# Earlier loads of a tail, casts on other engines and a new order of steps in a fused attention and MLP kernel

## The chip, the cores and the metric

The kernel runs on one core of a Trainium2 chip. The core has a matrix engine (TensorE, PE in the profile), a vector engine (VectorE, DVE), a scalar engine (ScalarE, ACT), a general engine (GpSimd, POOL) and a sync engine (SyncE, SP) that here only issues transfers. Transfers are carried by 16 DMA engines. The metric is the device time of one execution in microseconds; the median of several executions is given.

## The reference

There are 8 batches of 8 heads, 576 tokens and 64 dimensions a head. Attention is causal with a window of 64 tokens, and its output, with the heads side by side (512 numbers a token), goes through a layer norm, an MLP with a hidden width of 2048, and a residual add.

```python
scores = scale * np.matmul(q, k.transpose(0, 1, 3, 2))
mask = (rel >= 0) & (rel < 64)               # rel = query position - key position
attn = softmax(np.where(mask, scores, -1e9))
x = np.matmul(attn, v)                       # then heads side by side: (8, 576, 512)
xn = (x - mu) / np.sqrt(var + 1e-06) * g_ln
out = x + np.maximum(xn @ w_ch1, 0.0) @ w_ch2
```

## The kernel before

**Groups.** The 576 tokens of a batch are cut into 512 and a tail of 64. The kernel has nine groups of 512 tokens: group g below 8 is the first 512 tokens of batch g, and group 8 gathers the eight tails, two batches to a block of 128 tokens. A block of the attention is called a step j (0 to 3); of group 8, step i is "tail i", with the last 64 tokens of batches 2i and 2i+1. While the MLP of group g runs, the attention of batch b = g + 1 is computed between its matmuls, and in groups 6 and 7 that of the tails too.

**Units and slots.** `mlp_units` returns the matmul units of a group's MLP in order. After unit i the kernel runs what was put into slot i by `at(i, f, ...)`; within a slot, calls run in the order in which they were put there. Everything is written in program order and each engine works through its own list in that order, so a step that waits holds up all that stands behind it on its engine. Groups 2 to 8 have 16 units of the first MLP matrix (L437, `hps`, one chunk of 128 hidden units each) and 14 units of the second (L515, banks `wX`, `wY`, `wZ`), which use sums of the hidden activations (`presum`, L427) and of W2 (`t_weights`, L415). Group 0 splits the first matrix partly by halves of the tokens (L474, `hph`), and so does group 1; their second matrix is plain (L488 and L450, `ch`).

**An attention step.** `s_mm` makes the scores on TensorE (L292) and their exp on ScalarE (L312 or L306); `s_mask` multiplies by the mask on VectorE (L319); `b_step` makes the product with v on TensorE (L335) and, on VectorE, the division by the row sums and the statistics (L338 to L345); `r_step` makes 1/sqrt(var) on ScalarE (L354, L355); `z_step` normalizes on VectorE (L365). z is then transposed, either on TensorE with a copy on ScalarE (`zt_step`, L379 and L382) or by a DMA transpose from SP's queue (`x_step`, L390). `bz(i, ...)` puts `b_step`, `r_step` and `z_step` into slots i, i+1 and i+2.

**q, k and v.** SP loads them in fp32 (L78 to L90, v at L152). They are cast to fp16 by `cp`, on GpSimd (L131) or on ScalarE (L129), and q and k are transposed: for batches 0 to 2 on TensorE (`t_main`, L233, with the copy out at L225 on ScalarE or L227 on VectorE), for the others by DMA from SP's queue (`x_main`, L245 and L251). `pace(t)` is a copy of one column on GpSimd; it makes GpSimd wait until t is written, so that casts come no earlier than a wanted point. A shifted copy of v (`vB`) is made by two DMAs from GpSimd's queue (`make_vB`, L180, L181), for batch 1 by casts (`vB_cur`, `vB_prev`).

**The tails.** `load_tail(i, 0)` issues four loads of q and k from SP (L101, L103), `load_tail(i, 1)` two loads of v (L108). `cast_tail(i, part, act)` casts q (part 0), k (1) or v (2), on ScalarE where act is true. `x_tail(i)` issues two DMA transposes from SP (L261 for q, `tqT`; L262 for k, `tkT`). The staging buffers of q and k exist twice (tail 2 takes that of tail 0), that of v once, so a v load waits for the cast of the v before. The table `TAILS` says in which slot of groups 6 and 7 each of these steps stands. The scores of tail 1 stand in slot 27 of group 6, those of tails 2 and 3 in slots 9 and 13 of group 7.

**W1 and W2.** W1 is loaded in eight pieces (`w1_load`) and cast to fp16 with the norm's gain multiplied in (`w1_cast`: L205 on ScalarE, L207 on VectorE or GpSimd). Pieces 4 to 7 are staged in the space of W2. W2 is loaded in eight pieces through four buffers (`w2_load`, L212) and cast on GpSimd (`w2_cast`, L217); each cast frees the buffer for a later load. `rest_of_loads` holds these casts and loads and those of batch 1 and the q and k of batch 2.

Of the kernel before, what the change touches and what calls it, by code (L numbers as in the profile page):

```python
# [18 lines left out]
def kernel(  # L19
# [10 lines left out]
    nc = tc.nc  # L30
# [92 lines left out]
    def cast_qk(b, half):  # L123
        for x in range(2):
            cast_q(b, x, half)
# [7 lines left out]
    def cast_q(b, x, half, act=False):  # L133
        t = qk32.pop((b, x, half))
        dst = p_in.tile([128, 8, 2, D], FP16, tag=f"qk16_{x}", name=f"qk16_{x}_{b}_{half}")
        qk16[(b, x, half)] = dst
        if b >= NPE and x == 1:
            cp(act, dst[:, :].rearrange("p a e d -> p (a e d)"), t)
            return
        j = 2 if b < 2 else 4  # L140
        cp(act, dst[:, :].rearrange("p (a j) e d -> p a e j d", j=j),
           t[:, :].rearrange("p (a e j d) -> p a e j d", e=2, j=j, d=D))
# [5 lines left out]
    def load_v(b, c0, c1):  # L148
        if c0 == 0:
            v32[b] = p_in.tile([128, 4, H, D], FP32, tag="v32", name=f"v32_{b}", bufs=1)  # L150
        for c in range(c0, c1):
            nc.sync.dma_start(  # L152
                out=v32[b][:, c],
                in_=v[b, :, 128 * c:128 * c + 128, :].rearrange("h s d -> s h d"),
            )

    def cast_v(b, c0, c1, act=False):
        cp(act, vA[b][:, c0:c1, :, 0:D], v32[b][:, c0:c1])
# [50 lines left out]
    def w2_load(i):  # L209
        t = p_wst.tile([128, 2, DM], FP32, tag="wld", name=f"w2s_{i}")  # L210
        wst[("w2", i)] = t
        nc.sync.dma_start(  # L212
            out=t, in_=moe_w_ch2[256 * i:256 * (i + 1), :].rearrange("(c p) d -> p c d", p=128),
        )

    def w2_cast(i):
        nc.gpsimd.tensor_copy(out=w2s[:, 2 * i:2 * i + 2, :], in_=wst.pop(("w2", i)))  # L217
# [152 lines left out]
    def pace(t):  # L370
        nc.gpsimd.tensor_copy(out=tok, in_=t)
# [280 lines left out]
    load_qk(1, 0)  # L652
    for i in range(4):
        w2_load(i)
    cast_qk(1, 0)

    def rest_of_loads():
        for i in range(8):
            w2_cast(i)
            if i < 4:  # L660
                w2_load(i + 4)
        load_v(1, 0, 2)
        cast_v(1, 0, 1)
        cast_v(1, 1, 2)
        load_qk(1, 1)
        load_v(1, 2, 4)
        cast_qk(1, 1)
        cast_v(1, 2, 3)
        cast_v(1, 3, 4)
        load_qk(2, 0)  # L670
        load_qk(2, 1)

    def tail_casts(i, act, *us):
        return tuple((u, cast_tail, i, part, act) for part, u in enumerate(us))

    TAILS = {
        6: ((0, load_tail, 0, 0), (0, load_tail, 0, 1), (6, load_tail, 1, 0), *tail_casts(0, False, 8, 9, 10),
            (10, x_tail, 0), (10, load_tail, 1, 1), *tail_casts(1, True, 17, 18, 19), (18, x_tail, 1),
            (18, s_mm, 8, 0), (19, s_mask, 8, 0), (26, b_step, 8, 0),
            (18, load_tail, 2, 0), (20, load_tail, 2, 1), (20, load_tail, 3, 0),  # L680
            (27, s_mm, 8, 1), (28, s_mask, 8, 1)),
        7: (*tail_casts(2, False, 0, 1, 2), (2, load_tail, 3, 1), (3, x_tail, 2), *tail_casts(3, False, 4, 5, 8),
            (8, x_tail, 3), (2, b_step, 8, 1), (4, zt_step, 8, 0), (7, zt_step, 8, 1),
            (9, s_mm, 8, 2), (11, s_mask, 8, 2), (13, s_mm, 8, 3), (13, b_step, 8, 2),
            (15, s_mask, 8, 3), (17, zt_step, 8, 2), (20, b_step, 8, 3), (25, zt_step, 8, 3)),
    }
    for g in range(NGRP):
# [3 lines left out]
        def at(i, f, *a):  # L691
            slots[min(i, len(slots) - 1)].append((f, a))

        def bz(i, *p):
            at(i, b_step, *p)
            at(i + 1, r_step, *p)
            at(i + 2, z_step, *p)
# [23 lines left out]
        if g == 0:  # L721
            at(0, b_step, 0, 3)
            at(0, z_step, 0, 3)
            at(0, w1_cast, 2, 1, nc.scalar)
            at(0, w1_cast, 3, 1, nc.scalar)
            at(0, w1_cast, 3, 0, nc.scalar, 256, 512)
            at(7, rest_of_loads)
            at(1, zt_step, 0, 2)
            at(2, zt_step, 0, 3)
            for j in range(4):  # L730
                at(3 + j, w1_cast, 4 + j, 0, nc.vector)
                at(3 + j, w1_cast, 4 + j, 1, nc.scalar)
                at(10 + j, r_step, 0, j)
            at(11, t_main, 1, 0, 0, 1)
            at(12, t_main, 1, 1, 0, 1)
            at(17, s_mm, 1, 0)
            at(19, s_mask, 1, 0)
            at(20, s_mm, 1, 1)
            at(22, s_mask, 1, 1)
            at(30, vB_cur, 1, 0, 0)  # L740
            at(30, vB_prev, 1, 0, 1)
            at(32, vB_cur, 1, 1, 0)
            at(33, vB_prev, 1, 1, 0)
            at(33, b_step, 1, 0)
            at(35, b_step, 1, 1)
            at(36, r_step, 1, 0)
            at(37, z_step, 1, 0)
            at(38, r_step, 1, 1)
            at(38, z_step, 1, 1)
            at(41, zt_step, 1, 0)  # L750
            at(42, zt_step, 1, 1)
            at(43, t_main, 1, 0, 1, 0)
            at(44, load_v, 2, 0, 4)
            at(28, alloc_qkT, 2)
            at(28, cast_q, 2, 0, 0)
            at(29, cast_q, 2, 1, 0)
            at(29, make_vB_half, 1)
            at(41, lambda: pace(zT[1][:, 0, 0:1]))
            at(41, cast_q, 2, 0, 1)
            at(43, cast_q, 2, 1, 1)  # L760
        if g == 1:
            at(2, t_main, 1, 1, 1, 1)
            at(4, s_mm, 1, 2)
            at(5, s_mask, 1, 2)
            at(6, s_mm, 1, 3)
            at(7, s_mask, 1, 3)
            bz(7, 1, 2)
            bz(9, 1, 3)
            at(8, t_main, 2, 0, 0, 0)
            at(10, t_main, 2, 1, 0, 0)  # L770
            at(11, zt_step, 1, 2)
            at(13, t_main, 2, 0, 1, 0)
            at(14, zt_step, 1, 3)
            at(15, t_main, 2, 1, 1, 1)
            at(4, alloc_v, 2)
            at(4, alloc_vB, 2)
            for c in range(4):
                at(5 + c, cast_v, 2, c, c + 1)
            at(8, make_vB, 2)
            for j in range(4):  # L780
                at((17, 19, 21, 24)[j], s_mm, 2, j)
                at((18, 20, 22, 25)[j], s_mask, 2, j)
                bz((19, 21, 24, 27)[j], 2, j)
                at((22, 25, 28, 31)[j], zt_step, 2, j)
        if g > 0:
            if g == 1:
                for u, i, c in ((10, 1, 0), (11, 1, 1), (13, 2, 0), (14, 2, 1)):
# [26 lines left out]
        if 0 < g and b + 1 < B:  # L814
            n = b + 1
            e = 3 if g == 1 else 1
            at(e, load_qk, n, 0)
            at(e + 1, load_qk, n, 1)
            at(e + 4, load_v, n, 0, 4)
            if g == 1:  # L820
                at(10, alloc_qkT, n)
                for u, x, half in ((17, 0, 0), (19, 1, 0), (21, 0, 1), (23, 1, 1)):
                    at(u, lambda u=u: pace(hrTs[g][:, 2 * (u - 16), 256:257]))
                    at(u, cast_q, n, x, half)
                at(20, x_main, n, 0)
                at(24, x_main, n, 1)
                at(19, alloc_v, n)
                at(19, alloc_vB, n)
                for u, c, j in ((22, 0, 0), (23, 1, 0), (26, 2, 1), (28, 3, 2)):
                    at(u, (lambda j=j: pace(zT[b][:, 0, 128 * j:128 * j + 1])) if c % 2 == 0 else  # L830
                       (lambda j=j: pace(rss[(b, j)])))
                    at(u, cast_v, n, c, c + 1)
                at(28, make_vB, n)
            else:
                at(3, alloc_qkT, n)
                for u, x, half in ((16, 0, 0), (16, 1, 0), (17, 0, 1), (19, 1, 1)):
                    at(u, cast_q, n, x, half, True)
                at(18, x_main, n, 0)
                at(21, x_main, n, 1)
                at(18, alloc_v, n)  # L840
                at(18, alloc_vB, n)
                for c in range(4):
                    at(21 + c, cast_v, n, c, c + 1, True)
                at(25, make_vB, n)
# [37 lines left out]
```

## Time and profile before

| | us |
|---|---|
| median of 7 executions | 314.52 |
| lowest and highest | 311.74, 318.95 |
| the profiled execution, its own time | 314.01 |
| span of its profile | 312.3 |
| TensorE busy | 293.0 |
| VectorE busy | 192.5 |
| ScalarE busy | 187.7 |
| GpSimd busy | 84.9 |

The span runs from the first to the last instruction; about 1.7 us of the execution's time lie outside of it. The page's groups of instructions give a line, an engine, the operation with its tiles (output, then input), the count, the busy time, the mean of one in ns, and the idle time before them with what ended it:

```profile
L437 PE MATMUL hps<-zT,w1g 128*128 128x512 f16 x480 | 112.5, 382 | 0.9 <-ACT zT L382 0.7
L441 ACT ACTIVATE hrT<-hps 128x512 f16<-128x512 f32 x120 | 71.5, 596 | 45.2 <-PE hps L437 45.2
L319 DVE TENSOR_TENSOR pt<-pt,mask 128x1024 f16<-128x1024 f16 x32 | 22.9, 716 | 31.6 <-ACT pt L312 18.2
L131 POOL CAST qk<-qk 128x1024 f16<-128x1024 f32 x16 | 16.6, 1039 | 13.6 <-DMA qk<-in_q_dram 10.4
```

TensorE's matmuls overlap, so the mean of one is longer than its share of the time. The page's slices of the span (40 of 7.8 us each, a digit for tenths) show the clock that TensorE was granted and the share in which the DMA engines were busy:

```profile
PEclk9999999999999999999999999999999997999998
DMA  7999999999979977998999789979999993003004
```

The DMA engines are busy in almost every slice up to 258 us. One slice has a lower clock, that from 257.6 to 265.4 us.

### The profile page before, as it was taken

The page shows a single profiled execution, that of the slowest core. Times are in us where ns is not written, and L with a number is a line of the kernel's source. Part 1 is how long each engine was busy: PE and PEld are TensorE (multiplying, and loading weights), DVE is VectorE, ACT ScalarE, POOL GpSimd, SP SyncE. Part 2 cuts the span into 40 slices and gives each one's busy share as a digit, 9 for nine tenths or more (in the row PEclk, how much of TensorE's full clock was granted, in tenths as well). Part 3 has the DMA queues.
Part 4 walks back from the last instruction along what each step waited for, and adds up shares of the span by engine and source line. Part 5 has one row for each costly group of instructions (what it writes and reads, how often), then busy time and mean ns, then how long its engine had stood idle before and what let it go on. Part 6 is the DMA issues. An engine that isn't in the chain of part 4 may idle for free.

```text
span 312.3 us, 7262 instructions
## 1 busy us (share of the span) xinstructions
PE 293.0 (94%) x2939; PEld 186.1 (60%) x2939; DVE 192.5 (62%) x354; ACT 187.7 (60%) x367; POOL 84.9 (27%) x147
## 2 busy tenths in 40 slices
PE   5789998999999999999999999999999968999992
PEld 2446544856644478448745874596468634784582
DVE  0683328376885896479458927883798633862361
ACT  2699734747747874788488737974774465316500
POOL 3684765962551002200310040003130441000000
PEclk9999999999999999999999999999999997999998
DMA  7999999999979977998999789979999993003004
GB/s 178 259 385 342 320 263 271 296 302 225 201 143 262 221 95 141 321 217 123 133 322 217 120 163 334 188 132 219 230 159 151 243 233 65 2 2 134 0 12 124
DMA packets 135713, 60.49 MB, mean 194 GB/s; under 512 B 112784, under 2 KB 128656, under 8 KB 135680
## 3 DMA queue, kind: packets, MB, share of 16 engines
q1 hardware_dynamic: 131472, 48.12, 72.2%
q0 software_dynamic: 3216, 11.39, 12.3%
q10 hardware_dynamic: 992, 0.53, 0.7%
q8 instruction: 23, 0.38, 0.5%
q14 instruction: 10, 0.08, 0.1%
HBM read 38.80 MB, written 9.44 MB: 154 GB/s over the span
## 4 chain that ended last, share of the span: by engine, by line
PE 76%; DVE 8%; ACT 5%; SPq 4%; DMA 4%; issue 1%; POOL 0%; DVEq 0%
PE hps L437 33%; PE wX L515 14%; PE wZ L515 7%; PE hph L474 4%; PE xps L335 3%; PE ch L450 3%; PE sc L292 3%; PE wY L515 3%; PE ch L488 3%; DMA w1s<-in_moe_w_ch_dram 3%; SPq L152 2%; DVE stats L343 2%; DVE xn L341 2%; ACT hrT L479 1%; DVE pt L319 1%
## 5 line engine op out<-in xcount | busy, mean ns | idle before, releaser
L437 PE MATMUL hps<-zT,w1g 128*128 128x512 f16 x480 | 112.5, 382 | 0.9 <-ACT zT L382 0.7
L441 ACT ACTIVATE hrT<-hps 128x512 f16<-128x512 f32 x120 | 71.5, 596 | 45.2 <-PE hps L437 45.2
L437 PEld LDWEIGHTS <-w1g 128*128 128x128 f16 x480 | 45.1, 98 | 53.7 <-issue 6.7
L515 PEld LDWEIGHTS <-sw 128*128 128x128 f16 x448 | 43.5, 98 | 5.8 <-issue 0.8
L319 DVE TENSOR_TENSOR pt<-pt,mask 128x1024 f16<-128x1024 f16 x32 | 22.9, 716 | 31.6 <-ACT pt L312 18.2
L515 PEld LDWEIGHTS <-hrT 128*128 128x128 f16 x336 | 32.2, 98 | 5.5
L180 POOL DMA_DIRECT2D vB<-vA x6 | 3.2, 533 | 99.1 <-ACT vA L129 74.3
L398 POOL DMA_DIRECT2D out_dram<-osb x20 | 13.2, 662 | 56.8 <-DVE osb L533 48.8
L343 DVE BATCH_NORM_STATS2 stats<-xn 128x6 f32<-128x512 f32 x36 | 25.0, 695 | 1.2
L341 DVE TENSOR_TENSOR xn<-xps,rcp 128x512 f32<-128x512 f32 x36 | 24.9, 691 | 1.2
L427 DVE TENSOR_TENSOR sw<-hrT 128x1024 f16<-128x1024 f16 x28 | 18.8, 672 | 10.3 <-ACT hrT L441 10.3
L306 ACT ACTIVATE pt<-sc 128x512 f16<-128x512 f32 x40 | 23.7, 593 | 1.7
L474 PE MATMUL hph<-zT,w1g 128*128 128x256 f16 x192 | 23.9, 273 | 0.5 <-POOL w1g L207 0.4
L354 ACT ACTIVATE rs<-mv,epst 128x1 f32<-128x1 f32 x36 | 10.7, 298 | 22.1 <-DVE mv L345 22.1
L365 DVE TENSOR_SCALAR z<-xn,mv,rs 128x512 f16<-128x512 f32 x32 | 18.8, 590 | 6.0 <-ACT rs L355 5.8
L312 ACT ACTIVATE pt<-sc 128x512 f16<-128x512 f32 x32 | 17.4, 596 | 8.2 <-PE sc L292 8.2
L335 PEld LDWEIGHTS <-pt 128*64 128x64 f16 x576 | 12.4, 110 | 14.0 <-issue 5.6
L131 POOL CAST qk<-qk 128x1024 f16<-128x1024 f32 x16 | 16.6, 1039 | 13.6 <-DMA qk<-in_q_dram 10.4
L533 DVE TENSOR_TENSOR osb<-wX,xn 128x512 f32<-128x512 f32 (+1 forms) x24 | 14.9, 619 | 8.4 <-PE wX L515 8.4
L474 PEld LDWEIGHTS <-w1g 128*128 128x128 f16 x192 | 17.8, 98 | 3.6 <-POOL w1g L207 0.8
L450 PE MATMUL ch<-w2s,hrT 128*128 128x512 f16 x80 | 19.8, 380 | 0.0
L382 ACT COPY zT<-ztp 128x512 f16<-128x512 f16 x21 | 12.3, 584 | 11.1 <-PE ztp L379 10.9
(83 smaller groups left out, 412.2 us busy)
## 6 DMA issues: line engine op xcount, KB each, us to landing
qk<-in_q_dram SPq DMA_DIRECT2D x16, 512.0 KB, 7.6
v<-in_v_dram SPq DMA_DIRECT2D x32, 256.0 KB, 6.2
w2s<-in_moe_w_ch_dram SPq DMA_DIRECT2D x12, 512.0 KB, 7.3
out_dram<-osb POOLq DMA_DIRECT2D x12, 512.0 KB, 7.6
qk<-in_k_dram SPq DMA_DIRECT2D x20, 256.0 KB, 7.6
qk<-in_k_dram SPq DMA_DIRECT2D x6, 512.0 KB, 6.6
w1s<-in_moe_w_ch_dram SPq DMA_DIRECT2D x4, 512.0 KB, 6.4
out_dram<-osb POOLq DMA_DIRECT2D x8, 256.0 KB, 5.6
```

Source lines behind the costliest of these rows:

```text
L306: nc.scalar.activation(out=pt[:, par].rearrange("k h w (p j) -> k (h w) p j", j=4), in_=sc[:, :].rearrange("k h w (j p) -> k (h w) p j", j=4),
L319: nc.vector.tensor_tensor(out=ptv, in0=ptv, in1=mb, op=ALU.mult)
L335: nc.tensor.matmul(out=xps[64 * r:64 * r + 64, h, :D + 1], lhsT=pt[:, par, hp, r, :], rhs=rhs, start=True, stop=True)
L341: nc.vector.tensor_tensor(out=xn, in0=xps[:, :, 0:D], in1=rcp_b, op=ALU.mult)
L343: nc.vector.bn_stats(out=stats, in_=xn.rearrange("p h d -> p (h d)"))
L365: nc.vector.tensor_scalar(out=z, in0=x, scalar1=mv[:, 0:1], scalar2=rss[(g, kb)][:, 0:1], op0=ALU.subtract, op1=ALU.mult)
L427: nc.vector.tensor_tensor(out=S[i], in0=a, in1=b, op=op)
L437: nc.tensor.matmul(out=hps, lhsT=w1g[:, kc, 128 * hc:128 * (hc + 1)], rhs=zT[g][:, kc, :], start=(kc == KCS[0]), stop=(kc == KCS[-1]),)
L441: nc.scalar.activation(out=hrT[:, hc, :], in_=hps, func=AF.Relu, bias=0.0, scale=1.0)
L450: nc.tensor.matmul(out=ch[kb], lhsT=hrT[:, hc, 128 * kb:128 * (kb + 1)], rhs=w2s[:, hc, :], start=(hc == 0), stop=(hc == NHC - 1),)
L474: nc.tensor.matmul(out=hps[:, e], lhsT=w1g[:, kc, 128 * hc:128 * (hc + 1)], rhs=zT[g][:, kc, 256 * half:256 * half + 256], start=(kc == KC ...
L515: nc.tensor.matmul(out=xyz[bank][t * two_banks][:, t], lhsT=lhsT, rhs=rhs, start=bool(first and (t == 0 or two_banks) and hc == 0), stop=( ...
```

## The change

It has three parts.

1. **Tail 2.** The load of q and k of tail 2 moves from slot 18 to slot 12 of group 6, on SP's queue between two DMA transposes of z of batch 7 and ahead of the transposes of tail 1. Its casts of q and k move from GpSimd in slots 0 and 1 of group 7 (each behind a `pace`) to ScalarE in slots 24 and 25 of group 6, and its transposes from slot 3 of group 7 to slot 25 of group 6, behind tail 2's v load and ahead of tail 3's loads. The cast of its v stays on GpSimd, in slot 0 of group 7 instead of 2. Tail 3's q and k loads move from slot 20 to 26 of group 6, its v load from slot 2 to 0 of group 7, and its casts from slots 4, 5 and 8 to 3, 4 and 6.
2. **W1.** Of the four `w1_cast` on ScalarE beside those on VectorE in slots 3 to 6 of group 0, two go to GpSimd. For that, the casts of batch 1's first half of q and k, which stand on GpSimd, move from ahead of group 0 into `rest_of_loads`, so that GpSimd has the two W1 casts first.
3. **Order.** In group 0, z of batch 1's first block moves up by one slot, ahead of VectorE's output add. In group 1, the last two TensorE transposes of batch 2's q and k, the scores, and all that follows from them stand one to two slots earlier, as do the casts of batch 3's v.

```diff
-    cast_qk(1, 0)
 
     def rest_of_loads():
+        cast_qk(1, 0)
         for i in range(8):
             w2_cast(i)
...
         6: ((0, load_tail, 0, 0), (0, load_tail, 0, 1), (6, load_tail, 1, 0), *tail_casts(0, False, 8, 9, 10),
-            (10, x_tail, 0), (10, load_tail, 1, 1), *tail_casts(1, True, 17, 18, 19), (18, x_tail, 1),
-            (18, s_mm, 8, 0), (19, s_mask, 8, 0), (26, b_step, 8, 0),
-            (18, load_tail, 2, 0), (20, load_tail, 2, 1), (20, load_tail, 3, 0),
+            (10, x_tail, 0), (10, load_tail, 1, 1), (12, load_tail, 2, 0), *tail_casts(1, True, 17, 18, 19),
+            (18, x_tail, 1), (18, s_mm, 8, 0), (19, s_mask, 8, 0), (20, load_tail, 2, 1), (26, b_step, 8, 0),
+            *tail_casts(2, True, 24, 25), (25, x_tail, 2), (26, load_tail, 3, 0),
             (27, s_mm, 8, 1), (28, s_mask, 8, 1)),
-        7: (*tail_casts(2, False, 0, 1, 2), (2, load_tail, 3, 1), (3, x_tail, 2), *tail_casts(3, False, 4, 5, 8),
-            (8, x_tail, 3), (2, b_step, 8, 1), (4, zt_step, 8, 0), (7, zt_step, 8, 1),
+        7: (*((i, f, *a) for i, f, *a in tail_casts(2, False, 0, 0, 0) if a[1] == 2), (0, load_tail, 3, 1),
+            *tail_casts(3, False, 3, 4, 6),
+            (6, x_tail, 3), (2, b_step, 8, 1), (4, zt_step, 8, 0), (7, zt_step, 8, 1),
...
-            at(7, rest_of_loads)
             at(1, zt_step, 0, 2)
             at(2, zt_step, 0, 3)
             for j in range(4):
                 at(3 + j, w1_cast, 4 + j, 0, nc.vector)
-                at(3 + j, w1_cast, 4 + j, 1, nc.scalar)
+                at(3 + j, w1_cast, 4 + j, 1, nc.gpsimd if j % 2 else nc.scalar)
                 at(10 + j, r_step, 0, j)
+            at(7, rest_of_loads)
...
-            at(37, z_step, 1, 0)
+            at(36, z_step, 1, 0)
...
-            at(13, t_main, 2, 0, 1, 0)
+            at(12, t_main, 2, 0, 1, 0)
+            at(13, t_main, 2, 1, 1, 1)
             at(14, zt_step, 1, 3)
-            at(15, t_main, 2, 1, 1, 1)
...
-                at((17, 19, 21, 24)[j], s_mm, 2, j)
-                at((18, 20, 22, 25)[j], s_mask, 2, j)
-                bz((19, 21, 24, 27)[j], 2, j)
-                at((22, 25, 28, 31)[j], zt_step, 2, j)
+                at((15, 17, 20, 23)[j], s_mm, 2, j)
+                at((16, 18, 21, 24)[j], s_mask, 2, j)
+                bz((18, 20, 23, 26)[j], 2, j)
+                at((21, 24, 27, 30)[j], zt_step, 2, j)
...
-                for u, c, j in ((22, 0, 0), (23, 1, 0), (26, 2, 1), (28, 3, 2)):
+                for u, c, j in ((21, 0, 0), (22, 1, 0), (25, 2, 1), (27, 3, 2)):
...
-                at(28, make_vB, n)
+                at(27, make_vB, n)
```

## The prediction

> **What bounds the kernel now.** I read the page first. Its chain of work that ended last gives TensorE three quarters of the span, so most of the time is matmul work that the change leaves alone. What can be won is what stands on the chain between matmuls, so the second view is that chain in order of time, the third the busy time by stage, the fourth the timelines of single queues. From the page:
>
> ```profile
> PE 76%; DVE 8%; ACT 5%; SPq 4%; DMA 4%; issue 1%; POOL 0%; DVEq 0%
> ```
>
> The chain between 228 and 285 us (start, length, what):
>
> ```profile
> 253.61 1.74 PE hps L437 x8
> 255.35 0.23 SPq L261
> 255.62 3.29 DMA tkT<-tk
> 258.90 0.04 issue
> 258.95 0.61 PE sc L292 x12
> 259.55 4.66 PE hps L437 x16
> ```
>
> TensorE arrives at the scores of tail 2 at 255.35 and starts them at 258.95: 3.6 us of nothing, the only long hole after 95 us. The 16 hps behind it took 4.66 us, where the same 16 took 3.66 at 219.71, and the scores took 0.61 instead of 0.34. The busy table shows why: the next to last figures of a row are the granted TensorE clock, the share of the DMA engines, and GB/s.
>
> ```profile
> 254.00:258.00 4.00, 1.33 (x7) 0.39 (x4) 0.69 (x1) 1.69 (x4) 2.00 (x4) 1.00 1.12 182
> 258.00:262.00 4.00, 3.05 (x23) 1.44 (x24) 0.00 (x0) 1.18 (x3) 0.45 (x1) 0.57 0.57 107
> ```
>
> So the hole costs 3.60 + 1.00 + 0.27 = 4.87 us. Its cause is in SP's timeline: tail 2's transposes stand behind tail 3's loads.
>
> ```profile
> 226.11 2.28 SPq L390 DMA_TRANSPOSE zT<-z  x1
> ...
> 232.92 2.82 SPq L390 DMA_TRANSPOSE zT<-z  x2
> ...
> 237.70 1.26 SPq L262 DMA_TRANSPOSE tkT<-tk  x1
> 239.01 1.32 SPq L101 DMA_DIRECT2D tq<-in_q_dram  x2
> 240.38 1.25 SPq L103 DMA_DIRECT2D tk<-in_k_dram  x2
> ...
> 251.10 1.33 SPq L108 DMA_DIRECT2D tv<-in_v_dram  x2
> 252.48 3.10 SPq L261 DMA_TRANSPOSE tqT<-tq  x1
> 255.62 1.30 SPq L262 DMA_TRANSPOSE tkT<-tk  x1
> ```
>
> The casts of tail 2 ended on GpSimd at 249.9, but SP waited until 251.08 for the buffer of tail 3's v, and the transposes came after it. The same chain between 14 and 60 us, then the ScalarE timeline there:
>
> ```profile
> 25.93 0.61 ACT w1g L205
> 26.54 0.49 ACT hrT L479
> ...
> 30.36 2.75 PE hps L437 x12
> ...
> 51.58 0.83 DVE z L365
> ```
> ```profile
> 45.31 0.62 ACT L225 CAST vB<-v 64x512 f16<-64x512 f32 x1 [3.75 <-DMA v<-in_v_dram]
> 47.34 1.26 ACT L225 CAST vB<-v 64x512 f16<-64x512 f32 x2 [1.41 <-DMA v<-in_v_dram]
> ```
>
> From 25.3 to 30.4 ScalarE alternates between relus and W1 casts and TensorE waits for its PSUM buffers; but at 45.3 and 47.3 the work waits for v of batch 1 from memory, which no faster ScalarE brings nearer.
>
> **Part 1, tail 2.** Removed from SP between 239.0 and 241.7: four loads (two tq, two tk, 2.62 us of issue). Added after zT's second transpose, whose issue ends near 234.5: the same four. Their buffers are free (tail 0's casts ended at 227.8). Now tail 2's transposes stand ahead of tail 3's loads. ScalarE gets a 128x512 cast (0.61) and a 128x1024 cast (1.05, both as for tail 1 at 231.83), placed behind the zT copy that ends at 239.9. The tk half lands at about 236.5 + 5.5 (what tail 1's tk took) = 242.0, so ScalarE is held until 243.1. Queued behind are the rs of tail 0 and the exp of tail 1's scores; ScalarE sits idle there for 4.33 us until 244.23, so the 1.66 us are hidden with 1.1 us to spare. GpSimd loses two casts and two pacing copies. SP then takes tail 2's v (to 243.5), tqT (2.3, the price of a first transpose behind loads at 226.11) and tkT (to 247.1, landed by about 249): wanted at 255.35, so the hole goes.
>
> What is late next? The four loads are moved ahead of zT's third transpose and tail 1's two. I take the analogous stretch: tail 1's tk loads were issued by 226.0, then came zT, tqT and tkT of tail 0, and tkT landed at 230.09 + 3.2 = 233.3, so 7.3 us after the last load's issue. In the changed order the loads end at 237.1, so tail 1's tkT lands at 244.4. TensorE wants it at 243.26: a new wait of 1.1 us. Bounds: if the transposes need only their issue time (1.3 + 1.5 + 1.26) and 3.2 for the last, 243.1 and no wait; if the first takes 3.10 as at 252.48, 1.9 us. Here a rule of the Trainium skill leans to the low end: "DMA: Bandwidth & Descriptors", HWDGE ordering, says that completion is not FIFO per issuing engine, so a transpose need not wait for loads ahead of it. In this trace the landing order did follow the issue order (tk at 230.6, zT 230.9), so I take 1.1; by the rule part 1 would give 4.9, by the row 3.8. A wait of 1.1 costs no clock here: the 0.8 us hole at 93.1 left it at 1.00.
>
> zT's third transpose lands near 242, wanted at 245.4. Tail 3: its loads go from 244.1 to 247.1–250; tk lands 5.9 us (the median of tk) after about 249.3, at 255.2, GpSimd casts it in 1.19 to 256.4, its tkT lands at 259.6. Wanted at 255.35 + 1.1 + 0.34 + 3.66 = 260.45: 0.85 in hand. If tk takes 7.8, the longest seen, 1.0 us of wait comes instead. Sum of part 1: 4.87 − 1.1 = 3.8.
>
> **Part 2, two W1 casts on GpSimd.** ScalarE loses two casts of 0.61. Replaying the two PSUM buffers with relu 0.6 and a matmul unit 0.87, hps chunk 9 starts at 29.8 instead of 30.36: 0.6 earlier. But the first product with batch 1's v waits for the cast that ends at 45.93, and TensorE started it at 46.09 with no gap: 0.1 of the 0.6 remains. GpSimd pays 1.85 each (its one 128x512 row of this operation; ScalarE's need is a third of that): free at 25.98, it ends at 29.7, and its next work, the cast of batch 1's q, waits for its load until 29.81. Cover 0.1 us; beyond it every us delays the W2 casts and, through the buffers that they free, v at 45.3. A rule speaks against this: "SBUF — State Buffer" of the skill, on the shared port pair, says that GpSimd and a VectorE operation in a two-port mode exclude each other for a whole instruction, and VectorE casts W1 at 26.19 and 27.60. By the rule GpSimd loses up to 2 × 0.5 and the part costs about 0.9. In the trace GpSimd's 128x256 form took 0.91 at 22.18 under VectorE work and 1.0 on average: no block seen. I take 0.1 gained, range −0.9 to +0.6.
>
> **Part 3, order of the last steps.** VectorE's z of batch 1's first block now precedes the output add: z at 50.94 instead of 51.58, and TensorE, which waited 0.44 us for it at 52.45, has it in time: 0.44 gained. In group 1, the transpose at 71.31 still waits for ScalarE's copy, so advancing it by one unit leaves 0.87 of L2 work to do later; the first attention product loses its 0.45 wait; the second waits 0.8 instead of 0.5 for VectorE's mask, because mv of the product before now ends later beside it; and the hole of 0.8 before 93.92 is covered by four L2 matmuls (0.97). Replayed unit by unit, group 2 starts 0.2 earlier beyond the 0.44; range −0.9 to +0.6. Batch 3's last transpose lands at 93.3, wanted at 94.3. After 95 the chain is TensorE's own up to 255, so these stay.
>
> Sum: 3.8 + 0.1 + 0.44 + 0.2 = 4.5 us. The profiled execution took 314.01 (span 312.3); the median shown is 314.52, and 314.52 − 4.5 = 310.0.
>
> **The rivals.** *All of the hole is won* (10%): tail 1's tkT is in time, as SP's issue times alone would have it; gain 5.6, 308.9, with the upper ends of parts 2 and 3 307.9. Against it: the DMA share is above 1 in most rows from 226 to 258. *The wait moves to tail 3* (15%): the DMA engines had no slack from 242 to 258 (1.12 to 1.26), so tail 3's tkT, behind all else, decides. It landed at 261.5 before; if it still does, TensorE waits 1 to 2 us at the next scores; gain 1.5 to 3, about 312.2. For it: tk of tail 3 is issued 3 us later than before. *GpSimd or VectorE give back the front* (8%): parts 2 and 3 at their lower ends cost 1.4 beyond my sum plus a longer wait at tail 1; 312.5 to 314. *Slower* (7%): tail 1's tkT late enough to reopen the hole one step earlier. If tk takes 7.8 us from 236.4, zT, tqT and tkT follow at 244.2 and land by 248: 4.8 us of wait at 243.26, and a hole that long halves the clock again (1.3). It decides from a landing at 247.7; at 251 the kernel is slower by over 1%, 318. Against it: SP has nothing else there, and transposes landed in 3.2.
>
> **How the numbers follow.** My forecast, 310.0, has 60%: part 1 between 2.9 and 4.9, so 308.8 to 311.4. The range 307.9 to 313.3 takes in the bounds of parts 2 and 3 and the second and most of the third rival, and leaves out the slower one. About 1% is what a measurement of this kernel can tell from no change: 311.4 is that line. Faster: 0.56 of the forecast's 0.60, the first rival's 0.10, 0.02 of the second, 0.68; slower 0.07; the rest, 0.25, within 1%.
>
> **What would show it.** Right: no tkT wait at tail 2's scores, granted clock 1.00 throughout 240 to 270, a wait near 1 us at tail 1's scores, z of batch 1 before the add, hps chunk 9 half a us earlier and v at 45.3 as before. Wrong: a hole over 3 us anywhere after 240, ScalarE's cast of tk ending after 244.2, or v of batch 1 landing later than 46.

## The result and the profile after

The change took 312.99 us in the median of 27 executions (310.55 to 316.41), the kernel before 315.72 in the median of 64 (311.50 to 319.96). The ratio is 0.9946, with a 95% interval of 0.9923 to 0.9969: 1.7 us faster (1.0 to 2.4) where 4.5 were forecast. The ratio, here and below, is of the fast executions alone, which leaves out those more than about 1.5% above the shortest of their kernel, so it does not follow from the medians of all executions, which differ by 2.7 us. The profiled execution of the change took 310.81 us, which is near the short end of its own times, with a span of 309.1; stages are compared below between profiles, gains between times.

First the page of the change: the clock in 40 slices, and the shares of the chain that ended last.

```profile
PEclk9799999999999999999999999999999999999997
PE 64%; DMA 13%; DVE 10%; SPq 6%; ACT 3%; issue 2%; POOL 1%; ACTq 0%; POOLq 0%; DVEq 0%
```

The slow slice at 258 us is gone; the lower clock in the second slice lies ahead of the first `hph`, which starts at 19.91 us (before at 19.96). But transfers have gone up from 4% to 13% of the chain, VectorE from 8% to 10%, at the cost of TensorE's share. The rise of the transfers has two places: between 226 and 266 us they make up 17.2 us of the chain (before 3.3), and between 20 and 55 us a load of W2 and one of v are new in it. First the later place, in the chain of the change in order of time (start, length, what):

```profile
241.20 3.27 DMA tkT<-tk
244.51 0.45 PE sc L292 x16
...
250.63 5.97 DMA tk<-in_k_dram
...
257.79 3.13 DMA tkT<-tk
260.97 0.41 PE sc L292 x16
```

Two score products now stand behind a transpose: that of tail 1 at 244.51 and that of tail 3 at 260.97. Tail 2 is in no such line. TensorE's own timeline gives the waits as 1.57 us for tail 1, none for tail 2 (256.59), and 0.32 for tail 3. SP's timeline shows the order that makes them:

```profile
234.27 1.33 SPq L101 DMA_DIRECT2D tq<-in_q_dram  x2
235.64 1.91 SPq L103 DMA_DIRECT2D tk<-in_k_dram  x2
237.65 2.15 SPq L390 DMA_TRANSPOSE zT<-z  x1
...
241.20 1.26 SPq L262 DMA_TRANSPOSE tkT<-tk  x1
...
243.87 1.79 SPq L261 DMA_TRANSPOSE tqT<-tq  x1
245.75 1.77 SPq L262 DMA_TRANSPOSE tkT<-tk  x1
247.57 1.73 SPq L101 DMA_DIRECT2D tq<-in_q_dram  x2
249.34 3.60 SPq L103 DMA_DIRECT2D tk<-in_k_dram  x2
```

Tail 2's transposes are issued by 247.5, 9 us before they are wanted. The price is above them: tail 1's `tkT` goes out at 241.20 behind the four loads and a transpose of z, and lands at 244.47. The busy table has the place where the hole was (PE busy, then the others; the last three figures are clock, DMA share, GB/s):

```profile
254.00:258.00 4.00, 4.00 (x37) 1.90 (x35) 0.69 (x1) 2.95 (x6) 2.02 (x5) 1.00 1.14 218
258.00:262.00 4.00, 3.68 (x46) 1.79 (x45) 2.84 (x4) 3.36 (x6) 1.04 (x1) 1.00 0.40 69
```

TensorE is busy for 4.00 and 3.68 of each 4 us instead of 1.33 and 3.05, at the full clock. ScalarE's timeline shows the cast that the forecast had to hide:

```profile
241.78 1.04 ACT L129 CAST tk<-tk 128x1024 f16<-128x1024 f32 x1 [1.15 <-DMA tk<-in_k_dram]
```

The cast of `tk` ends at 242.8, ahead of the limit of 244.2 that the forecast gave. Now the front. In ScalarE's timeline v's first cast starts at 45.30, as before (45.31), and in TensorE's the first transpose of z at 51.85 has no wait any more. The chain's two new transfers are a load of W2 (7.08 us, from 29.91) and behind it the load of v that the casts at 47.34 wait for:

```profile
39.11 8.20 DMA v<-in_v_dram
```

A piece of the chain is not yet a wait. TensorE's timeline shows the wait, at the second product with v, before and after:

```profile
48.02 0.19 PE L335 MATMUL xps<-vB,pt 128*64 128x65 f16 x1 [0.36 <-ACT vB L225]
```
```profile
48.01 0.19 PE L335 MATMUL xps<-vB,pt 128*64 128x65 f16 x1 [0.37 <-ACT vB L225]
```

It waits for v's cast in both, and starts at the same time.

VectorE's pieces of the chain in group 1 (54.8 to 94 us) add up to 11.3 us, before 8.3. VectorE's timeline before (z, then a mask):

```profile
81.48 0.55 DVE L365 TENSOR_SCALAR z<-xn,mv,rs 128x512 f16<-128x512 f32 x1
...
83.80 0.66 DVE L319 TENSOR_TENSOR pt<-pt,mask 128x1024 f16<-128x1024 f16 x1
```

The same in the change (and the mask ahead of the first z), with GpSimd's casts of batch 3 and TensorE's products behind the masks:

```profile
79.82 0.66 DVE L319 TENSOR_TENSOR pt<-pt,mask 128x1024 f16<-128x1024 f16 x1
80.50 1.16 DVE L365 TENSOR_SCALAR z<-xn,mv,rs 128x512 f16<-128x512 f32 x1
...
83.36 1.41 DVE L319 TENSOR_TENSOR pt<-pt,mask 128x1024 f16<-128x1024 f16 x1
```
```profile
79.85 1.53 POOL L131 CAST qk<-qk 128x1024 f16<-128x1024 f32 x1
...
83.18 1.04 POOL L131 CAST qk<-qk 128x1024 f16<-128x1024 f32 x1
```
```profile
80.53 0.22 PE L335 MATMUL xps<-vB,pt 128*64 128x65 f16 x1 [0.70 <-DVE pt L319]
...
84.82 0.22 PE L335 MATMUL xps<-vB,pt 128*64 128x65 f16 x1 [0.56 <-DVE pt L319]
```

The operations are the same, and z takes 0.61 us longer and the mask 0.75 (the z behind it 0.96 instead of 0.69). z at 80.50 lies beside the cast that started at 79.85 (which itself took 1.53 instead of 1.04, having started under a mask), the mask at 83.36 beside the one from 83.18. TensorE waits 0.56 us for that mask; before, it found the third mask ready. The hole ahead of group 2 is gone, as forecast; before and after:

```profile
93.92 0.81 PE L437 MATMUL hps<-zT,w1g 128*128 128x512 f16 x3 [0.67 <-ACT zT L382]
```
```profile
93.60 1.03 PE L437 MATMUL hps<-zT,w1g 128*128 128x512 f16 x4
```

Even so, from the first `hph` of group 1 (54.47) to group 2 (93.60) it is 39.13 us, before 38.83. So in this pair of profiles the front wins 0.62 us (group 1 starts at 54.47 instead of 55.09), group 1 loses 0.30, and the stretch from group 2 to tail 3's scores wins 2.86 (167.37 instead of 170.23): 3.2 together, the difference of the spans.

### The profile page after: what moved, and what is told of

Read it like the earlier page. It is cut to its first block, busy times and chain, and to the rows that moved or that the text cites. A ratio compares the mean times of both kernels' runs of the same rounds, so it can differ in the third digit from the quotient of the medians.

```text
span 309.1 us, 7262 instructions
## 1 busy us (share of the span) xinstructions
PE 292.1 (94%) x2939; PEld 186.2 (60%) x2939; DVE 193.8 (63%) x354; ACT 188.6 (61%) x367; POOL 87.5 (28%) x145
## 4 chain that ended last, share of the span: by engine, by line
PE 64%; DMA 13%; DVE 10%; SPq 6%; ACT 3%; issue 2%; POOL 1%; ACTq 0%; POOLq 0%; DVEq 0%
PE hps L437 27%; PE wX L515 12%; PE wZ L515 6%; PE hph L474 5%; PE ch L450 4%; PE xps L335 3%; DMA w1s<-in_moe_w_ch_dram 3%; PE sc L292 3%; DMA v<-in_v_dram 3%; PE wY L515 2%; SPq L152 2%; DMA w2s<-in_moe_w_ch_dram 2%; DMA tkT<-tk 2%; DMA tk<-in_k_dram 2%; DVE stats L343 2%
## 5 line engine op out<-in xcount | busy, mean ns | idle before, releaser
L437 PE MATMUL hps<-zT,w1g 128*128 128x512 f16 x480 | 111.3, 379 | 0.2
L131 POOL CAST qk<-qk 128x1024 f16<-128x1024 f32 x16 | 17.7, 1111 | 9.9 <-DMA qk<-in_q_dram 5.9
```

Source lines behind the costliest of these rows:

```text
L437: nc.tensor.matmul(out=hps, lhsT=w1g[:, kc, 128 * hc:128 * (hc + 1)], rhs=zT[g][:, kc, :], start=(kc == KCS[0]), stop=(kc == KCS[-1]),)
```

## The experiments

Three questions: what each part is worth, where each part gives something back, and whether a version without the losses is faster. Where no other count is given, a ratio is from 15 to 22 executions beside 36 to 59 of the kernel before. "Stage A" is from group 2's first matmul to tail 3's scores, "stage B" from group 1's first `hph` to group 2, both from one profiled execution.

### One part at a time

**Part 1 alone**, in the kernel before:

```diff
-            (18, load_tail, 2, 0), (20, load_tail, 2, 1), (20, load_tail, 3, 0),
+            (10, x_tail, 0), (10, load_tail, 1, 1), (12, load_tail, 2, 0), *tail_casts(1, True, 17, 18, 19),
...
+            *tail_casts(2, True, 24, 25), (25, x_tail, 2), (26, load_tail, 3, 0),
```

> Part 1 alone on the kernel before. Theory A (the gain is all part 1's: the hole at tail 2's scores goes and shorter waits at tail 1's and tail 3's scores stay, 1.6 and 0.3 us): 2.5 to 3.3 us faster than before, the kernel changed in all its parts no faster than this one. Theory B (parts 2 and 3 carry a good share, part 1 being mostly eaten by new waits): 0 to 1 us faster. In the profile A wants a wait for tkT of 1 to 2 us before tail 1's scores and a granted clock of 1.00 after 250 us.

Measured 313.73, ratio 0.9927 (0.9892 to 0.9961): 2.3 us faster than before (1.2 to 3.4). Stage A is 167.43 us, before 170.23; the waits are 0.86 at tail 1, none at tail 2, 1.09 at tail 3. Stage B is 38.37 (38.83 and 38.39 in two profiles of the kernel before).

**The change without part 1**, the table of tails as before:

```diff
...
-            *tail_casts(2, True, 24, 25), (25, x_tail, 2), (26, load_tail, 3, 0),
+            (18, load_tail, 2, 0), (20, load_tail, 2, 1), (20, load_tail, 3, 0),
...
```

> Parts 2 and 3 without part 1. Theory A (parts 2 and 3 gain 0.44 from the earlier z and lose about as much in group 1): within 0.5 us of before, with the hole of 3 to 4 us at tail 2's scores and the lower clock after it as before. Theory B: 1 to 2 us faster.

315.15, ratio 1.0033 (1.0005 to 1.0061). Parts 2 and 3 together cost 1.0 us (0.2 to 1.9) instead of gaining 0.74. The hole at tail 2 was 4.37 us, stage B 39.14.

**The new order of group 1 alone**, in the kernel before:

```diff
...
-                at((17, 19, 21, 24)[j], s_mm, 2, j)
-                at((18, 20, 22, 25)[j], s_mask, 2, j)
...
+                at((15, 17, 20, 23)[j], s_mm, 2, j)
+                at((16, 18, 21, 24)[j], s_mask, 2, j)
...
```

> The kernel before with only the new order of group 1's last steps. If that order is what made parts 2 and 3 cost 1.0 us together: mask of batch 2 1.40 instead of 0.66, 39.1 to 39.6 us from the first hph of group 1 to group 2 (before 38.4 to 38.8), 0.6 to 0.9 us slower than before, ratio 1.002 to 1.003. If the loss came from the front: the same as before within 0.2.

316.71, ratio 1.0036 (1.0009 to 1.0063): 1.1 us slower (0.3 to 2.0). Stage B is 39.14, with a mask of 1.41 and z of 1.16 and 0.96.

**The front alone**: the two W1 casts and the moved z, in the kernel before.

```diff
...
-                at(3 + j, w1_cast, 4 + j, 1, nc.scalar)
+                at(3 + j, w1_cast, 4 + j, 1, nc.gpsimd if j % 2 else nc.scalar)
...
-            at(37, z_step, 1, 0)
+            at(36, z_step, 1, 0)
```

> The kernel before with only the two W1 casts on GpSimd and z of batch 1 ahead of the output add, neither part 1 nor the new order of group 1. By the durations in the profiles (16 hps 0.24 shorter, 40 hph 0.2 shorter, first transpose of z 0.5 earlier after the product): 0.7 to 0.9 us faster than before, ratio 0.997 to 0.998. If GpSimd's casts give the front back: the same or up to 0.6 slower, ratio 1.000 to 1.002.

315.05, ratio 0.9991 (0.9964 to 1.0019): 0.3 us faster, from 1.1 faster to 0.6 slower. The order of group 1 is thus the part that loses; that the front loses is not shown, and most of the gain expected of it is not shown either.

**The change without part 2**, all four casts on ScalarE:

```diff
-                at(3 + j, w1_cast, 4 + j, 1, nc.gpsimd if j % 2 else nc.scalar)
+                at(3 + j, w1_cast, 4 + j, 1, nc.scalar)
```

> The change with its two W1 casts put back on ScalarE (8 W1 casts of that loop: 4 VectorE, 4 ScalarE). If part 2 is worth what its own place showed (the 16 hps behind them 3.61 instead of 3.85 us, the 40 hph 4.74 instead of 4.96) and none of it is covered, 0.4 to 0.6 us slower than the change, about 312.7 to 313.5. If it is covered by the wait for v of batch 1, as the prediction had it: the same as the change within 0.2. If GpSimd's port use costs the front (the rival on GpSimd and VectorE), 0.5 to 0.9 faster. In all cases the wait at tail 1's scores stays near 1.3 and group 1 keeps its 39.1 to 39.6 from first hph to group 2.

313.25, ratio 0.9946 (0.9917 to 0.9975), the same ratio as the change. In the profile the stretch from the start of the 40 `hph` to the first L2 matmul (L488) took 13.06 us, with part 2 12.60, so that half a microsecond is won there; in the times it can't be seen. This front begins between 24.2 and 27.5 us from one profiled execution to the next, whatever the kernel, which is more than part 2 can bring.

**The change without the new order of group 1**, and the change once more:

```diff
...
-                at((15, 17, 20, 23)[j], s_mm, 2, j)
...
+                at((17, 19, 21, 24)[j], s_mm, 2, j)
...
```

> The change without its new order in group 1 (part 1, the W1 casts and the earlier z stay). Theory A (the new order costs about 0.5 us because VectorE's mask and z collide with GpSimd's casts of batch 3): 0.4 to 0.8 us faster than the changed kernel, the mask and z of batch 2 back at 0.7 and 0.55 us, group 2 starting near 93.3. Rival (the order gains what the forecast gave it): 0.2 us slower than the changed kernel.

> The changed kernel once more, beside the others on the same chip and for a second profile. Theory A: 2 to 3 us faster than before, with tkT waits of 1 to 2 us at tail 1's and up to 1 us at tail 3's scores again. Theory B (the first profile was a lucky execution): longer waits there, 3 us and more together.

Six executions each: 311.35, ratio 0.9855 (0.9798 to 0.9912), and 312.01, ratio 0.9862 (0.9812 to 0.9912). The repetition of the change lies below the interval of its main result, so ratios of six executions are compared only with each other here; these two can't be told apart. The traces can: stage B is 38.77 without the new order and 39.67 with it. Over all profiles on record in which nothing else was done to group 1, it is 38.4 to 38.8 with the old order (nine profiles) and 39.1 to 39.7 with the new one (eight).

### What holds VectorE in group 1

**Casts at their old place.** The casts of batch 3's q and k are paced by a column of the hidden activations on GpSimd. In the change, without another edit, two of the four casts wait for an earlier column, so that they come elsewhere relative to the masks:

```diff
-                    at(u, lambda u=u: pace(hrTs[g][:, 2 * (u - 16), 256:257]))
+                    at(u, lambda u=u: pace(hrTs[g][:, {17: 2, 19: 4, 21: 8, 23: 14}[u], 256:257]))
```

> The changed kernel with GpSimd's casts of batch 3's k (first half) and q (second half) paced by a hidden chunk one earlier, away from VectorE's masks and z. Theory A (VectorE's mask of 1.41 us and z of 1.16 us in the new order are collisions with these casts): the mask returns to 0.7 us and z to 0.55 us, group 1's second half to the start of group 2 shrinks by 0.5 to 0.7 us. Rival (they are long for another reason): both stay long.

VectorE's timeline of this kernel:

```profile
81.57 0.55 DVE L365 TENSOR_SCALAR z<-xn,mv,rs 128x512 f16<-128x512 f32 x1
...
83.89 0.66 DVE L319 TENSOR_TENSOR pt<-pt,mask 128x1024 f16<-128x1024 f16 x1
```

Mask and z are back at their durations of before, in the new order of steps, and stage B is 38.51 instead of 39.1 to 39.7. So the overlap with the casts is the loss, not the order itself. Freed from that, the order brings nothing either: 38.51 is what the old one gives (38.4 to 38.8). The time, 312.14 with a ratio of 0.9891 (0.9838 to 0.9945) in six executions, is too wide to add to this.

**A GpSimd operation that only writes.** Batch 3's casts of q and k on GpSimd become memsets, so this kernel leaves out batch 3's q and k:

```diff
...
+        if b == 3:
+            nc.gpsimd.memset(dst, 0.125)
+            return
```

> The changed kernel with GpSimd's casts of batch 3's q and k replaced by memsets of the same tiles, which read nothing (it leaves out batch 3's q and k). Theory A (the collision is between two readers of SBUF): the mask returns to 0.7 us and z to 0.55 us although GpSimd is as busy at the same places. Rival (any GpSimd work there lengthens them): the mask of 1.4 us stays.

One execution, 311.15. VectorE's and GpSimd's timelines (L325, L371 and L138 are the mask, z and a memset in this kernel's lines):

```profile
81.66 1.18 DVE L371 TENSOR_SCALAR z<-xn,mv,rs 128x512 f16<-128x512 f32 x1
...
84.54 0.66 DVE L325 TENSOR_TENSOR pt<-pt,mask 128x1024 f16<-128x1024 f16 x1
```
```profile
81.00 0.95 POOL L138 MEMSET qk<- 128x1024 f16 x1
...
84.33 0.95 POOL L144 MEMSET qk<- 128x1024 f16 x1
```

The mask at 84.54 lies inside the memset that started at 84.33 and takes its 0.66; z at 81.66 starts inside the other one and takes 1.18. So the mask, which reads two tensors from SBUF, is held by a GpSimd operation that reads, not by one that only writes; z, with one large input, is held by both. This is what the Trainium skill states in "SBUF — State Buffer", on the shared port pair: an operation with two SBUF inputs contends only with a GpSimd operation that reads, one in a two-port mode (it names `tensor_scalar` among those that can enter it) with any, for the whole instruction. TensorE did not wait for the third mask here, and stage B was 38.52: in this one execution z's extra 0.6 us alone cost nothing, so TensorE's wait of 0.56 in the change came only with the mask's 0.75 on top.

### Where the hole of tail 2 goes

**The order on SP's queue alone.** Tail 2's loads and GpSimd casts stay as before. Its transposes move from slot 3 of group 7 to slot 1, and tail 3's loads of q and k, which stood in slot 20 of group 6, come behind them:

```diff
-            (18, load_tail, 2, 0), (20, load_tail, 2, 1), (20, load_tail, 3, 0),
+            (18, load_tail, 2, 0), (20, load_tail, 2, 1),
...
-        7: (*tail_casts(2, False, 0, 1, 2), (2, load_tail, 3, 1), (3, x_tail, 2), *tail_casts(3, False, 4, 5, 8),
+        7: (*tail_casts(2, False, 0, 1, 2), (1, x_tail, 2), (1, load_tail, 3, 0), (2, load_tail, 3, 1), *tail_casts(3, False, 4, 5, 8),
```

> The kernel before with only SP's order at tail 2 turned round: tail 2's loads and GpSimd casts stay where they were, its two transposes are issued ahead of tail 3's loads. If the order alone made the hole: tail 2's tkT lands by about 254.5, no wait there, clock 1.00; tail 3's loads go 9 us later and its tkT is late by 2 to 3 us, so 1.5 to 2.5 us faster than before. If the early loads and ScalarE's casts are needed: tail 2 still waits 1 us or more (GpSimd's casts end at 249.9) and the sum of the waits stays at 3 us, the same as before within 0.5.

315.66, ratio 1.0038 (1.0006 to 1.0070). TensorE's timeline shows the scores of tails 2 and 3, the busy table the clock behind them:

```profile
256.43 0.41 PE L292 MATMUL sc<-tqT,tkT 64*128 64x64 f16 x16
...
264.32 0.61 PE L292 MATMUL sc<-tqT,tkT 64*128 64x64 f16 x16 [3.83 <-DMA tkT<-tk]
```
```profile
262.00:266.00 4.00, 1.68 (x34) 1.25 (x35) 0.42 (x2) 0.60 (x1) 1.04 (x1) 0.61 0.35 66
```

Tail 2 no longer waits, and the whole hole stands at tail 3, with its drop of the clock. The first branch of the expectation had the place right and the sum wrong: the wait was not 2 to 3 but 3.83 us, and nothing was won. Turning the order is thus not enough: with loads and casts where they were, the sum of the waits stays. In the change the early loads and casts come with the order; which of these two is needed was not tried apart.

**A second profile of the kernel before:**

> A second profile of the kernel before, to see how far the hole at tail 2's scores repeats: 3.6 to 4.4 us (3.61 in the first profile, 4.37 in the change without part 1), with the clock down in the 4 us behind it, and group 2 to tail 3's scores 170.2 to 171.8. If the hole were a chance of one execution: under 3 us.

317.60; the hole was 4.44 us, stage A 172.54. With the 4.37 of the change without part 1, the hole is 3.6 to 4.4 us, so the forecast's 3.61 is its low end.

**One transpose less ahead of tail 1.** z of block (7, 2) is transposed on TensorE instead of by SP:

```diff
-            if bj < 3:
+            if bg == 7 and bj == 2:
+                at(18, zt_step, bg, bj)
+            elif bj < 3:
```

> The changed kernel with z of batch 7's third block transposed on TensorE in slot 18 of group 6 instead of by SP's DMA transpose. Theory A (tail 1's scores wait because one more transpose stands between tail 2's loads and tail 1's transposes on SP): the wait before tail 1's scores falls from 0.7 to 1.6 us to under 0.3 us, TensorE pays 0.22 for the transposes; 0.3 to 1 us faster than the changed kernel unless tail 3's wait grows by as much. Rival (the DMA engines' throughput on tail 2's loads decides): the wait stays above 0.7 us.

311.66, ratio 0.9863 (0.9811 to 0.9914), six executions. The wait at tail 1 falls to 0.36, that at tail 3 rises to 1.16; stage A is 167.34, as in the change (167.37). Most of what was taken from one wait went to the other.

**Tail 3's loads one step earlier,** ahead of tail 2's transposes:

```diff
-            *tail_casts(2, True, 24, 25), (25, x_tail, 2), (26, load_tail, 3, 0),
+            *tail_casts(2, True, 24, 25), (25, load_tail, 3, 0), (25, x_tail, 2),
```

> The changed kernel with tail 3's q and k loads issued ahead of tail 2's transposes instead of behind them. Theory A (the wait at tail 3's scores comes from the late issue of its loads, and tail 2 has some 6 us to spare): the wait at tail 3's scores of 0.3 to 1.1 us goes, none comes at tail 2's; 0.3 to 1 us faster than the changed kernel. Rival (all of it is bound by the DMA engines, order only shifts the wait): tail 2's scores wait 1 us or more, or tail 3's wait stays.

310.49, ratio 0.9827 (0.9779 to 0.9876), six executions. No wait at tail 3, 1.17 at tail 1, stage A 166.65. The same edit to part 1 alone:

> The kernel before with part 1 alone, and in it tail 3's first loads ahead of tail 2's transposes. If tail 3's wait (1.09 us in the profile of part 1 alone) is what part 1 lacks against the forecast: no wait at tail 3, 0.9 to 1.3 at tail 1, 0.7 to 1.1 us under part 1 alone, ratio 0.989 to 0.991. If part 1 lacks it for another reason, which the profiled executions do not show: ratio 0.992 to 0.993 as part 1 alone.

312.40, ratio 0.9929 (0.9896 to 0.9963), the same as part 1 alone. Its tail 3 didn't wait either, but the times show no gain from that, so tail 3's wait of about 1 us is not what part 1 lacks in the times. (Its profiled execution, with a span of 312.8 us, is one of its long ones: TensorE waited 2.67 us at tail 1 with the clock down behind it. It is not counted below.)

**Is the wait at tail 1 steady?** Part 1 alone twice more, and the change once more, one execution each.

> Part 1 alone, one more profiled execution. If the wait at tail 1's scores is a spread that the forecast's single value missed: a wait other than the first profile's 0.86 at tail 1, above 1.5 in one of the next two executions, with the granted clock down behind it when it is above 2, and group 2 to tail 3's scores 168 to 170. If the wait is steady: 0.7 to 1.3 at tail 1 and 167.2 to 167.6.

> The same as for the run before it: above 1.5 us at tail 1's scores in one of the two if the wait is a spread; 0.7 to 1.3 in both if it is steady.

> The change once more: if the wait at tail 1 is a spread, it differs from 1.57 and 1.29, the earlier two, by over 0.5; if it is steady, 1.2 to 1.6 and group 2 to tail 3's scores 167.3.

They took 310.40, 312.25 and 311.51 us. TensorE's timelines of the two executions of part 1:

```profile
243.84 0.41 PE L292 MATMUL sc<-tqT,tkT 64*128 64x64 f16 x16 [0.29 <-DMA tkT<-tk]
...
260.56 0.41 PE L292 MATMUL sc<-tqT,tkT 64*128 64x64 f16 x16 [0.58 <-DMA tkT<-tk]
```
```profile
245.21 0.41 PE L292 MATMUL sc<-tqT,tkT 64*128 64x64 f16 x16 [2.03 <-DMA tkT<-tk]
...
262.44 0.41 PE L292 MATMUL sc<-tqT,tkT 64*128 64x64 f16 x16 [1.09 <-DMA tkT<-tk]
```

The same kernel waits 0.87 us in one execution and 3.12 in the other. The longer wait comes with a later SP: its loads of tail 1's k went out 128.8 us after group 2's start in the one, 130.1 in the other. The execution with the longer waits is also the longer one. The change's third profile has 0.80 and 0.89, so its sums in three profiles are 1.89, 1.81 and 1.69.

### The edits together

The change with three edits tried above, each against one loss: the paced columns, z of block (7, 2) on TensorE, tail 3's loads earlier.

```diff
+            *tail_casts(2, True, 24, 25), (25, load_tail, 3, 0), (25, x_tail, 2),
...
+            if bg == 7 and bj == 2:
+                at(18, zt_step, bg, bj)
...
+                    at(u, lambda u=u: pace(hrTs[g][:, {17: 2, 19: 4, 21: 8, 23: 14}[u], 256:257]))
```

> The change with three edits together: z of block (7,2) transposed on TensorE, tail 3's first loads ahead of tail 2's transposes, and the pacing columns of batch 3's casts in group 1 set by the step that they stood at. Theory (one wait is left at tail 1, one at tail 3, and one loss in group 1, each its own): no wait at tail 3, at most 0.6 at tail 1, mask of group 1 0.66, 38.5 us from the first hph of group 1 to group 2; 1.3 to 1.9 us under the change, near 310.5. Rival (SP and the DMA engines have one sum of work there, so that what is taken from one wait goes to the next): the waits of tails 1, 2 and 3 still sum to 1.3 or more, and only group 1's 0.6 is gained, near 311.5.

310.24 in the median of 19 executions (308.21 to 312.97), ratio 0.9858 (0.9828 to 0.9888): 4.5 us faster than before (3.5 to 5.4), and the interval lies below that of the change's main result. The change without part 2, measured beside the same executions of the kernel before, gave 0.9946 (0.9917 to 0.9975), so the two differ clear of noise. What each of the three edits gave to this is not shown: six executions of tail 3's edit alone gave 0.9827, and stage A is 166.97 here, 166.65 with that edit alone. In the profile tails 2 and 3 don't wait, tail 1 still does, for 1.21 us; the mask is at 0.66 and stage B at 38.78. The theory's 0.6 at tail 1 was missed; the rival (all waits are one sum of 1.3 or more) is not clearly refuted by a sum of 1.21, against 1.7 to 1.9 in the change, but its 311.5 us was not what came.

## Why the prediction was wrong

Two steps of the sum failed: the new order of group 1, put at 0.2 us faster and measured 1.1 slower, and the waits that part 1 leaves, put at 1.1 us at tail 1 and at nothing at tail 3.

**Part 1: mechanism right, two terms of its sum mis-sized.** The forecast had the hole of 3.60, the clock of 1.00 and the longer scores of 0.27 go, and they went in every kernel with part 1 that was profiled at its usual length. The casts on ScalarE hid as told. The new wait at tail 1's scores came where it was put; its term was 1.1 us, and in six profiles of part 1 and of the change it was 0.29 to 2.03, 1.57 in the first of the change. (The forecast's upper bound of 1.9 comes to 1.6 by its own terms: 237.1 + 3.10 + 1.5 + 3.2 is 244.9, wanted at 243.26.) Of the two readings that it set side by side, the trace's row (1.1) came nearer than the rule (no wait). What the sum had at zero, with 0.85 us in hand, was tail 3's `tkT`: it was late by 0.3 to 1.1. Its tk was to land at 255.2 and landed at 256.6. The load itself cost what was said (5.97 us, 5.9 in the sum), but it was issued 1.3 us later: the pair's first issue began at 249.34, where the sum had the load's, and the second, which landed last, at 250.63. In profiles, stage A fell from between 170.2 and 172.5 (before, twice, and the change without part 1) to between 166.3 and 168.6; by the first pair it is 2.9 us, where 3.8 was forecast. In the times the gain is 2.3 us (1.2 to 3.4). The first profiled executions of the two kernels are among their shorter ones (part 1 alone: the shortest of 15; the change: the second of 27), and of the two repetitions of part 1 the longer has the longer waits. But in the change's three profiles the waits don't grow with the time (1.89, 1.69 and 1.81 us in executions of 310.81, 311.51 and 312.68), so that the length of the executions makes the difference is not shown.

**Part 2: right in its size; its cover was v, at a later product.** The hps chunk was to start 0.6 earlier, of which v would leave 0.1. The stretch was 0.5 us shorter (13.08 to 12.60). The forecast looked at the first product with v, for which v's cast had 0.16 us in hand. The second product waited for v already before the change (0.36 us), so that in this pair nothing is left: it starts at 48.02 and at 48.01. Where the front begins later, v is in time. In undelayed profiles this product follows the first L2 matmul by 10.24 us; of the eleven profiles with part 2, the six whose first L2 matmul starts at 37.69 or later show that figure, and in the five at 37.48 or earlier it comes 0.2 to 1.8 us later. GpSimd had only a small share in it: its casts took 1.56 and 1.86 us, batch 1's q was cast at 30.05 instead of 29.81, and v's first load was issued at 38.60 instead of 38.46. In the times nothing of part 2 is visible: 0.9946 with and without it.

**Part 3, z before the add: right.** From the first product to the first transpose of z it was 6.36 us before and 5.72 after, 0.6 shorter in this pair; 0.44 was forecast. Over all profiles it is 5.93 to 6.36 without this edit and 5.31 to 6.33 with it. In the times the whole front is worth 0.3 us, which can't be told from nothing.

**Part 3, order of group 1: a step that failed.** The forecast had it 0.2 us faster ("range −0.9 to +0.6", as a gain), and it is 1.1 us slower in the times (0.3 to 2.0), with a stage B of 39.1 to 39.7 instead of 38.4 to 38.8. What was named came: the first product's wait was lost, the second waited 0.70 us where 0.8 was forecast, and the hole ahead of group 2 was covered. What was not named is the third product's wait of 0.56 us, put at nothing because GpSimd's queue was not looked at. The replay moved VectorE's masks and z by one to two slots with their durations of before, while batch 3's casts of q and k kept their slots; so mask and z now lie on these casts, and the mask took 1.41 us instead of 0.66. The rule on the shared port pair was weighed for the W1 casts, where it did not decide, and left out here, where it did. The kernel with the paced columns shows this step alone: the durations go back, and with them 0.6 us.

**The sum.** By the times: part 1 −2.3, front −0.3, order of group 1 +1.1, together −1.5, measured −1.7. Against the forecast's −4.5, the order of group 1 is off by 1.3 us and part 1 by 1.5; each of these gains is known to about 1 us. (The forecast of 310.0 also subtracted from 314.52, the median of 7 executions; that of 64 is 315.72.) Of the rivals, the second (the wait moves to tail 3, gain 1.5 to 3) and the third (VectorE gives back, 312.5 to 314) both happened, each in part, and the measured 312.99 is nearest to the third. That rival had VectorE's loss in the front, though, and it came in group 1, so its number was met in part by luck. The one on the slower side did not come: the longest wait at tail 1 in an execution of the usual length was 2.03, not 4.8.

**Open.** Why part 1 gains less in the times than in most pairs of its profiles; and what shifts SP by over 1 us between executions of the same kernel.

## What to carry to other kernels

When steps of one engine are moved by a slot, lay the other engine of the shared port (GpSimd for VectorE) beside them again: durations taken from the old place hold only while their neighbours move along. When a wait on a queue is removed by putting its transfers earlier, price each transfer that is now behind them by a spread of issue times from the trace, not by the best one: here the sum of the waits fell from 4 to between 1 and 3 us and did not vanish. And a hole that is turned round by order alone is only moved, until something (here loads and casts in earlier idle time) really comes sooner.

## What the runs showed of the hardware

- A VectorE mask of 128x1024 in fp16 took 0.66 us alone and beside a GpSimd memset, 1.40 to 1.41 beside a GpSimd cast; z of 128x512 took 0.55 alone, 1.15 to 1.18 beside a cast and beside a memset. GpSimd's cast of 1.04 took 1.53 where it started under a mask.
- Not every wait cost clock: TensorE's waits of up to 2.03 us at tail 1 left it at 1.00. In one execution 2.67 us there (part 1 with tail 3's loads earlier) brought the window from 246 to 250 us to 0.59, and waits of 3.6 to 4.4 us a window of 4 us behind them to 0.50 to 0.61, also when the hole was moved to tail 3.
- From 215 us on, the issue of a DMA transpose from SP took 1.2 to 2.3 us behind another transpose and 1.2 to 3.8 us behind loads, over all profiles.
